# Attention and gated MLP in one kernel: attention output evicted into the natural order of tokens, and an output ring of six tiles

## The chip, the cores and the metric

The kernel runs on one core of one Trainium2 chip. The metric is the device time of one execution in microseconds (us); the median of six runs is compared. A core has five engines, each with its own queue of instructions, worked off in order: TensorE (PE; its weight loads are the row PEld), VectorE (DVE), ScalarE (ACT), GpSimd (POOL) and SyncE (SP, which here only issues DMAs). They meet through semaphores.

## The reference

Two stages. First a linear attention with decay over q, k, v of shape 4 x 8 heads x 768 tokens x 64, in blocks of 64 tokens:

```
for b in range(12):
    intra = einsum('bhic,bhjc->bhij', qb, kb) * Dmask      # Dmask[i,j] = lam**(i-j), i >= j
    intra = einsum('bhij,bhjd->bhid', intra, vb)
    inter = einsum('bhid,bhde->bhie', qb * lam_pow, kv_state)
    out[:, :, sl] = intra + inter
    kv_state = lam_block * kv_state + einsum('bhsd,bhse->bhde', kb_dec, vb)
```

Its heads are laid side by side as x (4 x 768 x 512). Then a gated MLP:

```
h = maximum(x @ w_in, 0)                     # 512 -> 1024
u, v = h[..., :512], h[..., 512:]
v_n = (v - mean(v)) / sqrt(var(v) + 1e-6)    # over the 512 features
v_s = einsum('ts,bsd->btd', w_spatial, v_n) + b_spatial[None, :, None]
out = (u * v_s) @ w_out                      # 4 x 768 x 512
```

## The kernel before

The work comes in twelve groups n of 256 tokens (3 for each of 4 batch entries), each with two chunks c of 128 tokens, and then in work per batch entry bb. Nothing is scheduled by a program: the string ORDER at the top is a list of tokens, walked once, and each token calls one function. The last letter is the engine (T PE, D DVE, A ACT, P POOL, S SP). What one engine does, it does in the order in which its letter comes up in that string.

For a group the tokens are: LK, LQ, LV load 512 KB of k, q, v (SP, line 191; a ring of three tiles each, so LK.8 refills the tile of group 5). Partition p gets the tokens 2p and 2p+1 of the group, so that one descriptor moves 512 contiguous bytes. KC, QC, QM and VD convert and scale them to bf16 (lines 174 to 178, 299 and 314, most on POOL). TK, TQ transpose on PE (L328), EK, EQ evict to kT, qT; from group 7 on DK, DQ do this as DMA transposes from SP. SC forms the scores (L369), MK masks them on DVE into a_sb (L373). KV adds k'v to the running state in PSUM bank 7 (L385), SS copies the state out, AV forms the attention output, transposed, in two banks (L406, L415). EX evicts it to xT (two instructions of 512 elements per partition, 22 of 24 on ACT). PV (L444) and PU (L490) multiply xT with the two halves of w_in, EV and EU apply the relu, giving v and u; BN, RA, RD, VN normalise v to vn.

Since a partition holds two neighbouring tokens, the attention output comes out of PSUM with all even tokens of a chunk ahead of the odd ones. Before the change this order is kept: xT, v and u have it, the spatial weight's transposes (WT, L502) pick every second column of w_spatial to match it on the contracted side, and the gated product puts u back in order.

For a batch entry: PW multiplies vn with the transposed spatial weight (L511), GB adds the bias on DVE into vsb (f32, two tiles, L516), GM forms the gated product gT = vsb * u (L522, 24 on POOL and 8 on DVE; 384 elements per partition each), PO multiplies with w_out (L528), EO evicts to o_sb, a ring of NO tiles (mostly ACT, line 174), ST stores 256 KB (SP, L551). The last tile is done in halves (PH, EH, SH).

Four more things matter for what follows. The 5 tokens GM.0.1.1, GM.0.0.0, GM.0.1.0, GM.0.0.1 and GM.0.3.1 on POOL come among KC.4, VD.3.1, QC.5, and are followed by VD.4.1, VD.4.0, VD.5.1, GT.0.2, WO, VD.5.0, QC.6, QM.7.1, VD.6.1, QM.7.0, VD.6.0, GM.0.2.0, KC.7. GT ("after", L253) copies one element of an input tile, so that what is behind it on POOL waits for that load; GT.0.2 reads the k tile of group 5. WO is the load of w_out, issued by POOL. On DVE the order there is MK.5.0, MK.5.1, GM.0.3.0, BN.3.1, BN.4.1, EQ.6, SS.4.1; on PE, PW.0.2.1 is followed by KV.5.0.

Of the kernel before, what the change touches and what calls it, by code (L numbers as in the profile page):

```python
# [9 lines left out]
BF16 = mybir.dt.bfloat16  # L10
I32 = mybir.dt.int32
AF = mybir.ActivationFunctionType
ALU = mybir.AluOpType
# [20 lines left out]
GM.0.1.0.P KV.3.0.T AV.3.0.0.T GM.0.0.1.P SC.4.1.2.T SS.3.0.A SC.4.0.5.T SY.3.0.D GB.0.2.0.4.D LV.6.2.S  # L34
KV.3.1.T AV.3.1.0.T QC.5.2.P MK.4.1.2.D PW.0.3.0.4.T EX.3.0.0.A EX.3.1.1.A GM.0.3.1.P MK.4.0.5.D TQ.5.0.T
LQ.7.2.S KC.5.2.A PU.3.1.1.T VD.4.1.P EQ.5.0.D SS.3.1.A TK.5.2.T VD.4.0.P GB.0.3.0.4.D PU.3.0.6.T EK.5.2.A
EU.3.1.1.D KV.4.0.T LV.7.2.S VD.5.1.P EU.3.0.6.A AV.4.0.0.T SS.4.0.D SC.5.0.4.T SY.4.0.D LK.7.2.S GT.0.2.P
WO.P SC.5.1.2.T VD.5.0.P KV.4.1.T MK.5.0.4.D AV.4.1.0.T PV.3.1.6.T LK.8.2.S EX.4.0.0.A QC.6.2.P MK.5.1.2.D
EX.4.1.1.A PV.3.0.5.T KC.6.2.A GM.0.3.0.D PV.4.1.0.T LQ.9.2.S EV.3.1.6.A TQ.6.3.T BN.3.1.D EV.4.1.0.A QM.7.1.P
TK.6.1.T PU.4.1.2.T BN.4.1.D VD.6.1.P PU.4.0.4.T EQ.6.3.D EU.4.1.2.A QM.7.0.P SS.4.1.D EV.3.0.5.A PW.0.2.1.6.T  # L40
EK.6.1.D EU.4.0.4.A VD.6.0.P KV.5.0.T GB.0.2.1.6.D AV.5.0.0.T SS.5.0.A SC.6.0.4.T GM.0.2.0.P SC.6.1.2.T
# [42 lines left out]
def kernel(  # L84
# [12 lines left out]
    nc = tc.nc  # L97
    P = 128
# [5 lines left out]
    NCH = DM // P  # L104
    NR = S // (2 * P)
    T2 = 2 * P
    Q64 = 64
    MID = S // 2
    NIN, NCA, NTR, NA, NX, NO, NVS = 3, 2, 2, 2, 3, 4, 2

    const = ctx.enter_context(tc.tile_pool(name="const", bufs=1))
    psum = ctx.enter_context(tc.tile_pool(name="psum", bufs=1, space=bass.MemoryType.PSUM))
# [1 line left out]
    def sb(shape, dt, name):  # L114
        return const.tile(shape, dt, name=name)

    def many(n, shape, dt, name):
        return [const.tile(shape, dt, name=f"{name}_{i}") for i in range(n)]
# [8 lines left out]
    ident = sb([P, P], BF16, "ident")  # L127
# [15 lines left out]
    wsp_raw = sb([P, NT, S], BF16, "wsp_raw")  # L143
# [10 lines left out]
    qT = many(NTR, [P, 4, 2, P], BF16, "qT")  # L154
    a_sb = many(NA, [P, 2, 2, 2, 2, P], BF16, "a_sb")
    s_sb = many(4, [P, 4, D], BF16, "s_sb")
    xT = many(NX, [P, 2, NCH, P], BF16, "xT")
    vh = many(2, [P, NT, DH], BF16, "vh")
    vn = many(2, [P, NT, DH], BF16, "vn")
    uT = many(2, [P, NCH, S], BF16, "uT")  # L160
    gT = many(2, [P, NCH, S], BF16, "gT")
    vsb = many(NVS, [P, S], FP32, "vsb")
# [6 lines left out]
    def bank(b, n=1):  # L169
        return ps[:, b] if n == 1 else ps[:, b:b + n]  # L170

    def copy(e, o, i):
        if e == "A":
            nc.scalar.activation(out=o, in_=i, func=AF.Copy)  # L174
        elif e == "D":
            nc.vector.tensor_copy(out=o, in_=i)  # L176
        else:
            nc.gpsimd.tensor_copy(out=o, in_=i)  # L178

    def vec(e):  # L180
        return nc.vector if e == "D" else nc.gpsimd
# [174 lines left out]
    def row(x):  # L356
        return slice(x * Q64, (x + 1) * Q64)

    def qv(n, o, u, c):
        return qT[n % NTR][row(o), u, :, c * Q64:(c + 1) * Q64]  # L360
# [30 lines left out]
        copy(e, s_sb[(2 * n + c) % 4].rearrange("p u d -> p (u d)"), bank(SB)[:, 0:4 * D])  # L391

    def a_v(e, n, part, b):
        po = bank(b, 2).rearrange("p z (c i x) -> p z c i x", c=2, i=2)
        r = n % NR
        a = a_sb[n % NA]

        def inter(c):
            if r == 0 and c == 0:
                return  # L400
            s = s_sb[(2 * n + c - 1) % 4]
            for i in range(2):
                for o in range(2):
                    for w in range(2):
                        u = 2 * i + w
                        nc.tensor.matmul(out=po[row(w), c ^ o, c, i], lhsT=s[row(o), u, :], rhs=qv(n, o, u, c),  # L406
                                         start=(c == 0 and i == 0), stop=False, skip_group_check=True)

        def intra(o):
            for i in range(2):  # L410
                for j in range(2):
                    for c in range(2):
                        for w in range(2):
                            u = 2 * i + w
                            nc.tensor.matmul(out=po[row(w), c ^ o, c, i], lhsT=vd[n % NCA][row(c), 4 * o + u, j, :],  # L415
                                             rhs=a[row(c), i, o, w, j, :],
                                             start=(r == 0 and o == 0 and i == 0 and j == 0),
                                             stop=(i == 1 and j == 1), skip_group_check=True)

        if part == 0:  # L420
            inter(0)
            intra(0)
        else:
            inter(1)
            intra(1)
# [2 lines left out]
        copy(e, apart[e], ps[0:1, b:b + 2, 0:1].rearrange("p z x -> p (z x)"))  # L428

    def e_x(e, n, z, b):  # L430
        xo = xT[n % NX]
        src = bank(b).rearrange("p (c i x) -> p c i x", c=2, i=2)
        flat = xo.rearrange("p c g x -> p (c g) x")
        if z == 0:
            dst = flat.rearrange("p (a i) x -> p a i x", i=2)[:, 0:4:3]
        else:
            dst = flat.rearrange("p (a i) x -> p a i x", i=2)[:, 1:3]
        copy(e, dst, src)


    def p_v(e, n, c, b):
        x = xT[n % NX]
        for g in range(NCH):
            nc.tensor.matmul(out=bank(b), lhsT=x[:, c, g],  # L444
                             rhs=win_sb[:, g, DH:DFF], start=(g == 0), stop=(g == NCH - 1))

    def relu(e, o, i):
# [34 lines left out]
                             scalar2=rstd[p2][:, t:t + 1], op0=ALU.subtract, op1=ALU.mult)  # L482

    def p_u(e, n, j, b):
        x = xT[n % NX]
        pu = bank(b).rearrange("p (f x) -> p f x", f=2)
        for f2 in range(2):
            f = 2 * j + f2
            for g in range(NCH):
                nc.tensor.matmul(out=pu[:, f2].rearrange("p (c x) -> p c x", c=2), lhsT=win_sb[:, g, f * P:(f + 1) * P],  # L490
                                 rhs=x[:, :, g, :], start=(g == 0), stop=(g == NCH - 1))

    def e_u(e, n, j, b):
        r = n % NR
# [3 lines left out]
    def w_t(e, s, b):  # L498
        pw = bank(b).bitcast(BF16)
        for a in range(NT):  # L500
            for m in range(2):
                nc.tensor.transpose(out=pw[row(m), a * P:(a + 1) * P], in_=wsp_raw[:, a, s * P + m:(s + 1) * P:2],  # L502
                                    identity=ident)

    def e_w(e, s, b):
        pw = bank(b).bitcast(BF16)[:, 0:S]
# [12 lines left out]
    def g_m(e, bb, f, i):  # L519
        HW = S // 2  # L520
        cols = slice(i * HW, (i + 1) * HW)
        vec(e).tensor_tensor(out=gT[bb % 2][:, f, cols].rearrange("p (a y m) -> p a y m", m=2, y=Q64),  # L522
                             in0=vsb[(bb * 4 + f) % NVS][:, cols].rearrange("p (a y m) -> p a y m", m=2, y=Q64),
                             in1=uT[bb % 2][:, f, cols].rearrange("p (a m y) -> p a y m", m=2, y=Q64), op=ALU.mult)

    def p_o(e, bb, t, b):
        for f in range(NCH):
# [21 lines left out]
    def st_o(e, bb, t):  # L549
# [3 lines left out]
    ops = dict(GT=after, lam=c_lam, WU=w_u, pos=c_pos, LB=l_b, LN=l_n, LL=l_l, LX=l_x, LT=l_t, idn=c_ident, msk=c_mask, mkc=c_mask2, WI=w_in, WS=w_sp, WO=w_out, BS=b_sp,  # L553
               LK=ld_k, LQ=ld_q, LV=ld_v, KC=k_c, QM=q_m, DK=d_k, DQ=d_q, QC=q_c, VD=v_d, TK=t_k, TQ=t_q, EK=e_k, EQ=e_q,
               SC=s_c, MK=m_k, KV=k_v, SS=s_s, AV=a_v, SY=s_y, EX=e_x, PV=p_v, EV=e_v, BN=b_n, RA=r_a, RD=r_d,
               VN=v_n, PU=p_u, EU=e_u, WT=w_t, EW=e_w, PW=p_w, GB=g_b, GM=g_m, PO=p_o, EO=e_o, ST=st_o, EH=e_h, SH=s_h, PH=p_h)
    with tc.manual_schedule():
        for token in ORDER.split():
# [32 lines left out]
```

## Time and profile before

| what | value |
|---|---|
| median of six runs | 152.56 us |
| the six runs | 147.62, 149.36, 149.83, 155.28, 155.66, 158.30 us |
| the profiled execution, its own time | 155.66 us |
| its span, first to last instruction | 154.0 us |
| mean granted PE clock | 0.965 of full |
| busy: PE, PEld, DVE, ACT, POOL | 140.6, 93.3, 105.2, 87.8, 74.5 us |
| chain that ended last: PE, DVE, ACT, issue, POOL | 77%, 10%, 5%, 4%, 2% |
| gated products L522, POOL | 24, mean 1098 ns, 26.0 us |
| gated products L522, DVE | 8, mean 1511 ns, 12.0 us |
| v scaling L314, POOL (512 elements) | 19, mean 1065 ns |
| bias add L516, DVE | 32, mean 550 ns |
| xT evictions L174, ACT | 22, mean 595 ns |
| output evictions L174, ACT, 512 elements | 22, mean 595 ns; 2.9 us waiting for output DMAs |
| spatial transposes L502, PE | 72 |
| DMA | 31.25 MB, mean 203 GB/s |

How to read it: [...]The chain of waits goes back from the last instruction to what released each step. A group is all instructions of one line, engine and form, with the mean duration and the idle time of the engine ahead of them. The timeline gives start, duration, engine, line and, in brackets, the idle time before and what ended it. Line 174, 176 and 178 are a copy helper (ACT, DVE, POOL), so its groups go by the tile written.

### The profile page before, as it was taken

What the parts mean: (1) busy time and instruction counts of PE and PEld (TensorE: products, weight loads), DVE (VectorE), ACT (ScalarE), POOL (GpSimd) and SP (SyncE); (2) the same over time, 40 slices, a digit from 0 to 9 for tenths busy, and PEclk for the clock granted to TensorE, in tenths of its full rate; (3) what the DMA queues carried; (4) which work ended last, traced back from release to release, by engine and by line L of the source; (5) the groups of instructions that cost most, each with busy time, mean ns of one, the idle gap of its engine ahead of it and who ended that gap; (6) DMA issues with size and microseconds to landing.
All of it is one profiled execution on the core that took longest, in us unless ns stands there. A gap on an engine that the chain in (4) does not pass through costs nothing.

```text
span 154.0 us, 4883 instructions
## 1 busy us (share of the span) xinstructions
PE 140.6 (91%) x2070; PEld 93.3 (61%) x2085; DVE 105.2 (68%) x191; ACT 87.8 (57%) x167; POOL 74.5 (48%) x84
## 2 busy tenths in 40 slices
PE   6998689999999999099999999999999999999990
PEld 4785546768766867083565657655676756565540
DVE  1468606988996799968566778885469888848301
ACT  3968238968406765035799824668373646942270
POOL 7445463205089999158244585574754102014910
PEclk9999969999999999857999999999999999999999
DMA  3999999999999999808699997988999000051355
GB/s 99 298 290 269 260 231 268 216 283 284 302 283 286 291 264 229 236 9 159 185 270 280 140 232 223 315 188 258 156 302 180 6 2 0 4 197 75 136 216 193
DMA packets 54152, 31.25 MB, mean 203 GB/s; under 512 B 11634, under 2 KB 51058, under 8 KB 54130
## 3 DMA queue, kind: packets, MB, share of 16 engines
q1 hardware_dynamic: 51600, 28.05, 73.2%
q0 software_dynamic: 2384, 2.75, 10.3%
q8 instruction: 16, 0.26, 0.7%
q10 hardware_dynamic: 146, 0.13, 0.2%
q14 instruction: 6, 0.05, 0.1%
HBM read 24.77 MB, written 6.29 MB: 202 GB/s over the span
## 4 chain that ended last, share of the span: by engine, by line
PE 77%; DVE 10%; ACT 5%; issue 4%; POOL 2%; DVEq 0%; POOLq 0%
PE ps L511 17%; PE ps L528 13%; PE ps L490 12%; PE ps L444 12%; PE ps L212 6%; DVE gT L522 4%; PE ps L415 4%; PE ps L369 3%; PE ps L385 3%; PE ps L328 3%; PE ps L406 2%; ACT kT L174 2%; ACT lq L234 2%; DVE a_sb L373 2%; POOL gT L522 1%
## 5 line engine op out<-in xcount | busy, mean ns | idle before, releaser
L522 POOL TENSOR_TENSOR gT<-vsb,uT 128x384 bf16<-128x384 f32 x24 | 26.0, 1098 | 33.2 <-DVE vsb L516 25.0
L511 PE MATMUL ps<-wt_sb,vn 128*128 128x384 bf16 x192 | 33.9, 327 | 0.0
L373 DVE TENSOR_TENSOR a_sb<-ps,m 128x1024 bf16<-128x1024 f32 x24 | 28.6, 1215 | 2.9 <-PE ps L369 2.5
L314 POOL TENSOR_TENSOR vd<-v_in,lv 128x512 bf16<-128x512 f32 x19 | 20.0, 1065 | 13.8 <-DMA v_in<-in_v_dram 8.8
L511 PEld LDWEIGHTS <-vn 128*128 128x128 bf16 x192 | 18.2, 98 | 11.9
L490 PE MATMUL ps<-xT,win_sb 128*128 128x256 bf16 x192 | 24.4, 273 | 0.0
L444 PE MATMUL ps<-win_sb,xT 128*128 128x512 bf16 x87 | 23.5, 397 | 0.8 <-issue 0.4
L516 DVE TENSOR_TENSOR vsb<-ps,bsp 128x384 f32<-128x384 f32 x32 | 17.2, 550 | 9.1 <-PE ps L511 9.0
L528 PE MATMUL ps<-wout_sb,gT 128*128 128x512 bf16 x86 | 22.1, 390 | 0.4 <-issue 0.2
L490 PEld LDWEIGHTS <-win_sb 128*128 128x128 bf16 x192 | 18.4, 98 | 4.7
L449 ACT ACTIVATE vh<-ps 128x512 bf16<-128x512 f32 x23 | 13.7, 597 | 12.5 <-PE ps L444 12.5
L174 ACT ACTIVATE o_sb<-ps 128x512 f32<-128x512 f32 (+1 forms) x23 | 13.1, 585 | 12.1 <-PE ps L528 9.2
L459 DVE BATCH_NORM_STATS2 st<-vh 128x6 f32<-128x512 bf16 x24 | 16.3, 681 | 3.1 <-ACT vh L449 3.0
L174 ACT ACTIVATE xT<-ps 128x512 bf16<-128x512 f32 x22 | 12.2, 595 | 7.7 <-PE ps L415 7.6
L444 PEld LDWEIGHTS <-xT 128*128 128x128 bf16 x96 | 9.1, 101 | 10.4 <-issue 1.7
L528 PEld LDWEIGHTS <-gT 128*128 128x128 bf16 x92 | 9.0, 100 | 9.9 <-issue 0.8
L212 PE MATMUL ps<-warm 128*128 128x256 bf16 x71 | 11.5, 317 | 2.7 <-DVE warm L210 1.3
L385 PE MATMUL ps<-vd,kc 64*64 64x64 bf16 x320 | 9.3, 201 | 5.0 <-DVE s_sb L176 3.7
L449 ACT ACTIVATE uT<-ps 128x512 bf16<-128x512 f32 x20 | 11.7, 595 | 2.9 <-PE ps L490 2.6
L299 POOL TENSOR_TENSOR qc<-q_in,lqn 128x512 bf16<-128x512 f32 x10 | 10.7, 1076 | 4.8 <-DMA q_in<-in_q_dram 4.7
L178 POOL CAST kc<-k_in 128x1024 bf16<-128x1024 f32 x6 | 6.2, 1036 | 13.9 <-DMA k_in<-in_k_dram 10.2
L385 PEld LDWEIGHTS <-kc 64*64 64x64 bf16 x320 | 7.8, 115 | 7.3 <-issue 6.9
(72 smaller groups left out, 184.6 us busy)
## 6 DMA issues: line engine op xcount, KB each, us to landing
k_in<-in_k_dram SPq DMA_DIRECT2D x12, 512.0 KB, 7.0
q_in<-in_q_dram SPq DMA_DIRECT2D x12, 512.0 KB, 7.8
v_in<-in_v_dram SPq DMA_DIRECT2D x12, 512.0 KB, 7.1
out_dram<-o_sb SPq DMA_DIRECT2D x23, 256.0 KB, 2.4
wsp_raw<-in_moe_w_spatial_dram POOLq DMA_DIRECT2D x2, 576.0 KB, 10.8
win_sb<-in_moe_w_in_dram POOLq DMA_DIRECT2D x2, 512.0 KB, 9.9
wout_sb<-in_moe_w_out_dram POOLq DMA_DIRECT2D x1, 512.0 KB, 10.1
bsp<-in_moe_b_spatial_dram SPq DMA_DIRECT2D x1, 384.0 KB
```

Source lines behind the costliest of these rows:

```text
L174: nc.scalar.activation(out=o, in_=i, func=AF.Copy)
L212: nc.tensor.matmul(out=bank(SB)[:, 4 * D:8 * D], lhsT=warm[:, 0:P], rhs=warm, start=(n < 0 and x == 0), stop=True, skip_group_check=True)
L314: vec(e).tensor_tensor(out=vd[n % NCA].rearrange("p (o i w) m d -> p o i (w m) d", o=2, i=2)[o], in0=v_in[n % NIN].rearrange("p (o i w) m ...
L373: nc.vector.tensor_tensor(out=a_sb[n % NA][:, i].rearrange("p o w j x -> p (o w) (j x)"), in0=bank(b, 2).rearrange("p o (w y) -> p (o w) y ...
L385: nc.tensor.matmul(out=pkv[row(o), u], lhsT=kc[n % NCA][row(c), u, m, o, :], rhs=vd[n % NCA][row(c), 4 * o + u, m, :], start=new and u == ...
L444: nc.tensor.matmul(out=bank(b), lhsT=x[:, c, g], rhs=win_sb[:, g, DH:DFF], start=(g == 0), stop=(g == NCH - 1))
L449: nc.scalar.activation(out=o, in_=i, func=AF.Relu)
L490: nc.tensor.matmul(out=pu[:, f2].rearrange("p (c x) -> p c x", c=2), lhsT=win_sb[:, g, f * P:(f + 1) * P], rhs=x[:, :, g, :], start=(g == ...
L511: nc.tensor.matmul(out=bank(b)[:, 0:HW], lhsT=vn[bb % 2][:, s, f * P:(f + 1) * P], rhs=wt_sb[:, s, i * HW:(i + 1) * HW], start=(s == 0), s ...
L516: nc.vector.tensor_tensor(out=vsb[(bb * 4 + f) % NVS][:, i * HW:(i + 1) * HW], in0=bank(b)[:, 0:HW], in1=bsp[:, i * HW:(i + 1) * HW], op=A ...
L522: vec(e).tensor_tensor(out=gT[bb % 2][:, f, cols].rearrange("p (a y m) -> p a y m", m=2, y=Q64), in0=vsb[(bb * 4 + f) % NVS][:, cols].rear ...
L528: nc.tensor.matmul(out=bank(b), lhsT=gT[bb % 2][:, f, t * P:(t + 1) * P], rhs=wout_sb[:, f, :], start=(f == 0), stop=(f == NCH - 1))
```

## The change

The attention output is put into the natural order of tokens when it is evicted to xT. AV's two banks have their chunks in another order (i, c in place of c, i), and each eviction reads its bank straight through and stores with an inner step of two bf16 elements, even tokens and odd tokens interleaved. PV and PU find their blocks of xT at other places. From there on v and u are in natural order: the spatial transposes take 64 neighbouring columns, and the gated products are plain, with all operands contiguous. The output ring grows from four tiles to six. One token, GT.0.2.P, is dropped from the order; all other tokens stay as they were (two lines of the string are wrapped differently).

```diff
-... LK.7.2.S GT.0.2.P
-WO.P SC.5.1.2.T ...
+... LK.7.2.S WO.P
+SC.5.1.2.T ...
-    NIN, NCA, NTR, NA, NX, NO, NVS = 3, 2, 2, 2, 3, 4, 2
+    NIN, NCA, NTR, NA, NX, NO, NVS = 3, 2, 2, 2, 3, 6, 2
-    xT = many(NX, [P, 2, NCH, P], BF16, "xT")
+    xT = many(NX, [P, 2, 2, 2, P], BF16, "xT")
     def a_v(e, n, part, b):
-        po = bank(b, 2).rearrange("p z (c i x) -> p z c i x", c=2, i=2)
+        po = bank(b, 2).rearrange("p z (i c x) -> p z c i x", c=2, i=2)
     def e_x(e, n, z, b):
-        xo = xT[n % NX]
-        src = bank(b).rearrange("p (c i x) -> p c i x", c=2, i=2)
-        flat = xo.rearrange("p c g x -> p (c g) x")
-        if z == 0:
-            dst = flat.rearrange("p (a i) x -> p a i x", i=2)[:, 0:4:3]
-        else:
-            dst = flat.rearrange("p (a i) x -> p a i x", i=2)[:, 1:3]
-        copy(e, dst, src)
+        copy(e, xT[n % NX].rearrange("p i c z (y m) -> p (i c) z m y", m=2)[:, :, z],
+             bank(b).rearrange("p (k m y) -> p k m y", k=4, m=2))
     def p_v(e, n, c, b):
-            nc.tensor.matmul(out=bank(b), lhsT=x[:, c, g],
+            nc.tensor.matmul(out=bank(b), lhsT=x[:, g % 2, c, c ^ (g // 2)],
     def p_u(e, n, j, b):
-        x = xT[n % NX]
+        x = xT[n % NX].rearrange("p i c z x -> p (i c z) x")
+                o, i = divmod(g, 2)
-                                 rhs=x[:, :, g, :], start=(g == 0), stop=(g == NCH - 1))
+                                 rhs=x[:, 4 * i + o:4 * i + 4 - o:3 - 2 * o], start=(g == 0), stop=(g == NCH - 1))
     def w_t(e, s, b):
-                nc.tensor.transpose(out=pw[row(m), a * P:(a + 1) * P], in_=wsp_raw[:, a, s * P + m:(s + 1) * P:2],
-                                    identity=ident)
+                c0 = s * P + m * Q64
+                nc.tensor.transpose(out=pw[row(m), a * P:(a + 1) * P], in_=wsp_raw[:, a, c0:c0 + Q64], identity=ident)
     def g_m(e, bb, f, i):
-        vec(e).tensor_tensor(out=gT[bb % 2][:, f, cols].rearrange("p (a y m) -> p a y m", m=2, y=Q64),
-                             in0=vsb[(bb * 4 + f) % NVS][:, cols].rearrange("p (a y m) -> p a y m", m=2, y=Q64),
-                             in1=uT[bb % 2][:, f, cols].rearrange("p (a m y) -> p a y m", m=2, y=Q64), op=ALU.mult)
+        vec(e).tensor_tensor(out=gT[bb % 2][:, f, cols], in0=vsb[(bb * 4 + f) % NVS][:, cols],
+                             in1=uT[bb % 2][:, f, cols], op=ALU.mult)
```

More of the change, by code (lines that the diff above doesn't have):

```diff
@@ L36 @@
 LQ.7.2.S KC.5.2.A PU.3.1.1.T VD.4.1.P EQ.5.0.D SS.3.1.A TK.5.2.T VD.4.0.P GB.0.3.0.4.D PU.3.0.6.T EK.5.2.A
-EU.3.1.1.D KV.4.0.T LV.7.2.S VD.5.1.P EU.3.0.6.A AV.4.0.0.T SS.4.0.D SC.5.0.4.T SY.4.0.D LK.7.2.S GT.0.2.P
-WO.P SC.5.1.2.T VD.5.0.P KV.4.1.T MK.5.0.4.D AV.4.1.0.T PV.3.1.6.T LK.8.2.S EX.4.0.0.A QC.6.2.P MK.5.1.2.D
+EU.3.1.1.D KV.4.0.T LV.7.2.S VD.5.1.P EU.3.0.6.A AV.4.0.0.T SS.4.0.D SC.5.0.4.T SY.4.0.D LK.7.2.S WO.P
+SC.5.1.2.T VD.5.0.P KV.4.1.T MK.5.0.4.D AV.4.1.0.T PV.3.1.6.T LK.8.2.S EX.4.0.0.A QC.6.2.P MK.5.1.2.D
 EX.4.1.1.A PV.3.0.5.T KC.6.2.A GM.0.3.0.D PV.4.1.0.T LQ.9.2.S EV.3.1.6.A TQ.6.3.T BN.3.1.D EV.4.1.0.A QM.7.1.P
```

## The prediction

> **What bounds the kernel now.** I read the chain of waits first. TensorE (PE) holds 77% of it. Then the line of granted clock in the 40 slices of 3.85 us:
>
> ```profile
> PE   6998689999999999099999999999999999999990
> PEclk9999969999999999857999999999999999999999
> ```
>
> PE is full in every slice from the seventh on except slice 17 (61.6 to 65.5 us), and in that slice and the two after it the clock dips. Two stretches from the table of windows (length, PE busy, PEld, DVE, ACT, POOL, then the clock):
>
> ```profile
> 65.00:69.00 4.00, 3.81 (x113) 3.26 (x114) 2.60 (x5) 1.12 (x4) 1.71 (x2) 0.50 0.06 16
> 69.00:73.00 4.00, 3.86 (x13) 1.60 (x13) 3.64 (x8) 2.27 (x6) 3.45 (x4) 0.69 0.81 149
> ```
>
> PE works there at half and at two thirds of its clock. So one place is worth reading closely. The chain, in order of time (start, us, what):
>
> ```profile
> 55.46 1.21 DVE a_sb L373
> 56.68 5.86 DVE gT L522
> 62.54 0.61 DVE st L459
> ...
> 64.07 0.66 DVE qT L354
> 64.73 0.34 DVE s_sb L176
> 65.07 0.04 issue
> 65.11 0.64 PE ps L385 x12
> ```
>
> One gated product on DVE (GM.0.3.0.D) takes 5.9 us. Queued behind it on DVE is SS.4.1.D, which empties PSUM bank 7, and PE can't start KV.5.0 before. The timeline of PE, with the idle time ahead in brackets:
>
> ```profile
> 65.11 0.64 PE L385 MATMUL ps<-vd,kc 64*64 64x64 bf16 x16 [3.73 <-DVE s_sb L176]
> ```
>
> This is PE's longest wait; from there to the end it has two of 0.22 and 0.16 us. What is special in that product? The other seven on DVE take 0.56 to 1.45 us (its group: min 559, median 786, max 5945 ns). The timelines of DVE and of POOL tell:
>
> ```profile
> 56.60 5.95 DVE L522 TENSOR_TENSOR gT<-vsb,uT 128x384 bf16<-128x384 f32 x1
> ```
>
> ```profile
> 56.05 1.04 POOL L178 CAST qc<-q_in 128x1024 bf16<-128x1024 f32 x1
> 57.05 1.03 POOL L299 TENSOR_TENSOR qc<-q_in,lqn 128x512 bf16<-128x512 f32 x1
> 58.05 1.03 POOL L314 TENSOR_TENSOR vd<-v_in,lv 128x512 bf16<-128x512 f32 x1
> 59.05 1.03 POOL L299 TENSOR_TENSOR qc<-q_in,lqn 128x512 bf16<-128x512 f32 x1
> 60.05 1.03 POOL L314 TENSOR_TENSOR vd<-v_in,lv 128x512 bf16<-128x512 f32 x1
> 61.05 1.07 POOL L522 TENSOR_TENSOR gT<-vsb,uT 128x384 bf16<-128x384 f32 x1
> 65.88 1.04 POOL L178 CAST kc<-k_in 128x1024 bf16<-128x1024 f32 x1 [3.75 <-issue]
> ```
>
> POOL has no gap from 42.93 to 62.12 us, and the DVE product ends 0.43 us after POOL does: it was shut out.
>
> [...] Before, the product reads u with an inner step of 64 bf16 elements, and takes 1.09 us for 384 elements (2.8 ns each), while the scaling of v, packed, takes 1.04 for 512 (2.03 ns)[...].
>
> **The change part by part.**
>
> *Products on POOL (24).* With all operands packed I take the rate of the v scaling: 384 x 2.03 = 0.78 us instead of 1.09, 0.31 saved[...]. 24 x 0.31 = 7.4 us of POOL. After 65 us PE doesn't wait for POOL, so this is worth nothing there; without that cover it would be 0.31 for each product. It matters for the run of work above. Five products lie between 42.93 and QM.7.1 (57.05): POOL comes to QM.7.1 by 5 x 0.31 = 1.55 earlier.
>
> *The token GT.0.2 dropped.* Its step on POOL was 0.13 us (54.12 to 54.25). So POOL is at QM.7.1 at 57.05 - 1.55 - 0.13 = 55.4. On SP the load LK.8 no longer waits for it (1.6 us in the waits of the queue), and LV.7, which waits for VD.4.0, goes about 1.5 earlier. The load of w_out moves as much; it must have landed by the first output product, and landed at 64.35 before (issued 54.25, 10.1 us).
>
> *What POOL meets at 55.4.* QM.7.1 needs q_in of group 7, issued by SP at 48.57 and landed 7.8 us later, at 56.4. The DMA was full then, so I let that time stand. So POOL sits idle from 55.4 to 56.4, where before it had 0.65 us in hand.
>
> *When DVE asks.* QC.5.2 on POOL ended at 50.14 and PE took its transposes at 50.20, having been free at 49.93; now QC.5.2 ends near 49.0: 0.27 earlier on PE. Next, KV.4.0 waited 0.25 (53.27) for VD.4.0 or the kT copy, ended 53.18 and 53.25: both come earlier, so another 0.25. The a_sb masks follow, and DVE asks for its product at 56.6 - 0.5 = 56.1. That falls in POOL's gap, with 0.3 us to spare. Then the product costs 0.56, POOL waits 0.2 for it, and the pause of PE goes.
>
> *What the pause is worth.* 3.73 us of idle PE, and its clock: over 65 to 73 us 4 x (1 - 0.50) + 4 x (1 - 0.69) = 3.24 us at most. Late next is VD.6.0 on POOL (done near 61.4), needed by KV.6.0 on PE near 62: hidden, narrowly.
>
> *Evictions into natural order (24, 22 on ACT).* I take 0.595 us as before. ACT's rate from two rows, (1022 - 595)/512 = 0.83 ns per element, leaves 427 ns to be doubled if stores of single bf16 elements ran at half rate: bounds 0 and +0.43 each, +9.4 us of ACT in all. TensorE's reads of xT stay in blocks of 128 elements: 0. DVE's products (8) at 0.56 equal the packed bias add at 0.55: 0.
>
> *Weight transposes.* 72 in 2.13 us, 30 ns each; the loads (110 ns, overlapping) become packed. Others of 128 columns take 0.45 to 0.62 us for 8. Taken as 0, bounds 0 and -0.3.
>
> *Output ring of six.* ACT waited 2.39 (139.2) and 0.46 (148.5) for output DMAs. PE had no gap around 139, and at the end the last matmul ends at 150.05 whatever ACT did before, its final eviction starting at 150.13: 0, bound -0.4.
>
> **Sum**, against the profiled execution (155.66 us, span 154.0 and 1.66 around it): 155.66 - 3.73 - 3.24 - 0.5 = 148.2; I say 148.3. That execution is in the upper half of the six runs (147.62 to 158.30, median 152.56). The lowest runs, 147.62 to 149.83, lie where this sum goes without the 0.5 (148.7): I read them as runs in which DVE already got its turn. So I expect few new lows, but most runs near the lows.
>
> **Rivals.**
> 1. [...]For it: 0.3 us of margin, worked out from several steps. If q_in lands before DVE asks, POOL runs on through QM.7.1 to GM.0.2.0, and ends at 56.4 + 4 x 1.0 + 0.8 = 61.2 instead of 62.1: 155.66 - 0.9 = 154.7; with runs of both kinds the median is 150 to 154.7.[...]
> 2. *The interleaved store is slow; the kernel ends slower.* Place: the two evictions at 49.04 us on ACT, ahead of KC.5.2, whose transposes feed the masks ahead of DVE's product. From +0.15 us each DVE asks after 56.4, [...]and the pause stays. At the full +0.43: 155.66 + 0.85 there + 0.85 for the pair at 24.05 ahead of the kT copy + some 1.3 for single ones (16 to 33 us) = 158.7.[...]
> 3. *The pause goes but a smaller wait takes its place*: w_out landing, or VD.6.0 held by a later q_in, costs PE 1 to 2 us: 150.
> 4. *Packed products are no faster on POOL*: only 0.13 is saved and POOL meets no gap; 155.5, counted with rival 1.
>
> **How the numbers follow.** Forecast 0.58 (own range 146.2 to 149.8); rivals 1 and 4 0.24; rival 2 0.12; rival 3 0.06. Faster by over 2% (below 149.5; 2% is about what a measurement of this kernel can tell from no change): 0.56 of the forecast, 0.04 of the rest, 0.60. Slower (above 155.6): 0.11 of rival 2 and 0.02 of rival 1, 0.13. Within: 0.27. The range runs from 146.2 to rival 1's 154.9 and leaves rival 2 out.
>
> **What would show it.** Products on POOL near 0.78 us; a gap on POOL before QM.7.1 near 56 us; the first DVE product under 1 us; no wait of PE above 0.5 us after 53 us and full clock from 61 us on; ACT evictions of xT at 0.60. Wrong if that product is again several us long, if xT's evictions are above 0.75 us, or if the packed products stay at 1.09.

## The result

The changed kernel takes 149.40 us (median of 35 runs, 147.39 to 157.11); the kernel before, now run 72 times, takes 149.07 (147.33 to 158.80), so the six runs shown ahead had set its median 3.5 us too high. The ratio of like runs is 1.0003, interval 0.998 to 1.0027: no change. A ratio of like runs compares only runs within 1.5% of the fastest of their kernel; it leaves out all runs above 153 us, which I count apart.

| | runs | above 153 us | median of the other runs |
|---|---|---|---|
| kernel before, all runs | 276 | 107 (39%) | 148.88 |
| changed kernel, both times that it was run | 57 | 8 (14%) | 148.77 |

Experiment 7 aside, I take the runs above 153 us as those in which PE paused: the three such executions that have a profile (155.66, 155.59 and 154.49 us) show the pause, and no profiled execution below 150 us does. So the pause of the kernel before is real, and rarer after the change. But the typical run of the kernel before never had it. (The profiled execution of the changed kernel took 148.49 us, span 146.8.)

The profile of the changed kernel shows the pause and the low clock behind it gone. Busy tenths and clock per slice (now 3.67 us each):

```profile
PE   6999589999999999999999999999999999999990
PEclk9999977999999999999999999999999999999999
```

No slice is empty but the last, and the clock doesn't dip after the first quarter. The two stretches, by the table of windows, are at full clock:

```profile
65.00:69.00 4.00, 4.00 (x51) 2.17 (x50) 3.13 (x12) 2.95 (x9) 1.68 (x2) 1.00 0.82 179
69.00:73.00 4.00, 3.89 (x105) 2.87 (x105) 2.48 (x8) 3.72 (x8) 0.36 (x1) 1.00 0.60 165
```

The chain around KV.5.0, which had waited 3.73 us (L506 is what L511 was):

```profile
58.21 1.75 PE ps L485 x16
59.96 0.97 PE ps L506 x6
60.93 0.30 PE ps L385 x12
```

PE goes from PW.0.2.1 into KV.5.0 without a gap. The product on DVE, and what POOL did around it:

```profile
56.15 0.55 DVE L517 TENSOR_TENSOR gT<-vsb,uT 128x384 bf16<-128x384 f32 x1
```

```profile
55.11 1.04 POOL L178 CAST qc<-q_in 128x1024 bf16<-128x1024 f32 x1
56.20 1.39 POOL L299 TENSOR_TENSOR qc<-q_in,lqn 128x512 bf16<-128x512 f32 x1
57.56 1.04 POOL L314 TENSOR_TENSOR vd<-v_in,lv 128x512 bf16<-128x512 f32 x1
```

DVE asks at 56.15, as POOL's QC.6.2 ends, and takes 0.55 us. Now QM.7.1 is the one that is held: 1.39 us instead of 1.03. The last two rows to compare are groups, with count, busy time and mean duration:

```profile
L517 POOL TENSOR_TENSOR gT<-vsb,uT 128x384 bf16<-128x384 f32 x24 | 21.8, 917 | 35.4 <-DVE vsb L511 26.6
L174 ACT ACTIVATE xT<-ps 128x512 bf16<-128x512 f32 x22 | 15.2, 743 | 6.8 <-PE ps L415 6.6
```

Products on POOL went from 1098 to 917 ns, the evictions to xT from 595 to 743. Span against span, 154.0 - 146.8 = 7.2 us: KV.5.0 starts 65.11 - 60.93 = 4.18 earlier, and the stretch behind it is 88.89 - 85.87 = 3.02 shorter, near the 3.24 that the low clock from 65 to 73 us could cost at most.

### The profile page after: what moved, and what is told of

The parts are those of the page before. It is cut to its first block, busy times and chain, and to the rows that moved or that the text cites. A ratio compares the mean times of both kernels' runs of the same rounds, so it can differ in the third digit from the quotient of the medians.

```text
span 146.8 us, 4879 instructions
## 1 busy us (share of the span) xinstructions
PE 137.7 (94%) x2070; PEld 91.5 (62%) x2085; DVE 99.1 (68%) x191; ACT 89.8 (61%) x167; POOL 70.7 (48%) x83
## 4 chain that ended last, share of the span: by engine, by line
PE 87%; ACT 6%; DVE 2%; issue 2%
PE ps L506 21%; PE ps L438 14%; PE ps L522 13%; PE ps L485 13%; PE ps L212 6%; PE ps L415 4%; PE ps L369 4%; PE ps L328 4%; PE ps L385 4%; PE ps L406 2%; ACT lq L234 2%; PE ps L498 1%; ACT kT L174 1%; ACT xT L174 1%; ACT vh L443 1%
## 5 line engine op out<-in xcount | busy, mean ns | idle before, releaser
L517 POOL TENSOR_TENSOR gT<-vsb,uT 128x384 bf16<-128x384 f32 x24 | 21.8, 917 | 35.4 <-DVE vsb L511 26.6
L506 PE MATMUL ps<-wt_sb,vn 128*128 128x384 bf16 x192 | 33.9, 327 | 0.0
L506 PEld LDWEIGHTS <-vn 128*128 128x128 bf16 x192 | 18.2, 98 | 11.9
L511 DVE TENSOR_TENSOR vsb<-ps,bsp 128x384 f32<-128x384 f32 x32 | 17.2, 550 | 9.8 <-PE ps L506 7.2
L438 PE MATMUL ps<-win_sb,xT 128*128 128x512 bf16 x87 | 22.8, 388 | 0.6 <-issue 0.2
L522 PE MATMUL ps<-wout_sb,gT 128*128 128x512 bf16 x86 | 21.4, 379 | 0.4 <-issue 0.2
L174 ACT ACTIVATE xT<-ps 128x512 bf16<-128x512 f32 x22 | 15.2, 743 | 6.8 <-PE ps L415 6.6
L299 POOL TENSOR_TENSOR qc<-q_in,lqn 128x512 bf16<-128x512 f32 x10 | 11.5, 1152 | 7.9 <-DMA q_in<-in_q_dram 6.1
L174 ACT ACTIVATE kT<-ps 128x1024 bf16<-128x1024 bf16 x6 | 6.1, 1020 | 8.1 <-PE ps L328 7.6
L415 PE MATMUL ps<-a_sb,vd 64*64 64x128 bf16 x384 | 11.0, 225 | 0.0
```

The source lines that it names most:

```text
L438: nc.tensor.matmul(out=bank(b), lhsT=x[:, g % 2, c, c ^ (g // 2)], rhs=win_sb[:, g, DH:DFF], start=(g == 0), stop=(g == NCH - 1))
L506: nc.tensor.matmul(out=bank(b)[:, 0:HW], lhsT=vn[bb % 2][:, s, f * P:(f + 1) * P], rhs=wt_sb[:, s, i * HW:(i + 1) * HW], start=(s == 0), s ...
L511: nc.vector.tensor_tensor(out=vsb[(bb * 4 + f) % NVS][:, i * HW:(i + 1) * HW], in0=bank(b)[:, 0:HW], in1=bsp[:, i * HW:(i + 1) * HW], op=A ...
L517: vec(e).tensor_tensor(out=gT[bb % 2][:, f, cols], in0=vsb[(bb * 4 + f) % NVS][:, cols], in1=uT[bb % 2][:, f, cols], op=ALU.mult)
L522: nc.tensor.matmul(out=bank(b), lhsT=gT[bb % 2][:, f, t * P:(t + 1) * P], rhs=wout_sb[:, f, :], start=(f == 0), stop=(f == NCH - 1))
```

## The experiments

Theory A: the pause is DVE shut out by POOL; the change makes it rarer; a run without it gains nothing. Theory B: runs without the pause would gain from faster products, but the slower evictions eat it. Every kernel was timed in five rounds beside the kernel before.

**1. The product taken off DVE, in the kernel before.**

```diff
-... KC.6.2.A GM.0.3.0.D PV.4.1.0.T ...
-... GM.0.2.0.P SC.6.1.2.T
+... KC.6.2.A PV.4.1.0.T ...
+... GM.0.2.0.P GM.0.3.0.P SC.6.1.2.T
```

> The kernel before with one change: the product GM.0.3.0 goes from DVE to POOL, behind GM.0.2.0[...]. [...]no run lies above 153 us (27 of 72 of the kernel before did), PE has no wait above 0.5 us after 53 us, and the lower group of times stays at 148.3 (ratio of like runs 0.997 to 1.003). If the pause comes of something else, a late load say, about one run in three stays above 153.

None of 22 runs lies above 153 us, where 24 of 60 of the kernel before, run beside it, did. The median of all is 148.90, the ratio of like runs 1.0017 (0.9987 to 1.0047). The pause hangs on this one instruction being on DVE.

**2. Products alone, in the kernel before.**

```diff
     def g_m(e, bb, f, i):
-        vec(e).tensor_tensor(out=gT[bb % 2][:, f, cols].rearrange("p (a y m) -> p a y m", m=2, y=Q64),
...
+        vec(e).tensor_tensor(out=gT[bb % 2][:, f, cols], in0=vsb[(bb * 4 + f) % NVS][:, cols],
+                             in1=uT[bb % 2][:, f, cols], op=ALU.mult)
```

> The kernel before with plain gated products alone: the reordering of u is left out, so even and odd tokens of v and u are mixed. Evictions stay at 0.595. Products on POOL near 0.91 us. Theory A: ratio of like runs 1.000 within 0.003, and clearly fewer than 3 of 8 runs above 153, since POOL now has a gap when DVE asks. Theory B: with no slower eviction the gain shows, ratio 0.995 to 0.997.

None of 14 runs above 153; median 148.87; ratio 0.9986 (0.9944 to 1.0028). Its products on POOL mean 918 ns, its evictions 595. The timelines of DVE and POOL in its profile:

```profile
56.92 0.55 DVE L522 TENSOR_TENSOR gT<-vsb,uT 128x384 bf16<-128x384 f32 x1
```

```profile
55.97 1.04 POOL L178 CAST qc<-q_in 128x1024 bf16<-128x1024 f32 x1
57.55 1.04 POOL L299 TENSOR_TENSOR qc<-q_in,lqn 128x512 bf16<-128x512 f32 x1 [0.54 <-DMA q_in<-in_q_dram]
```

POOL is through with QC.6.2 at 57.01, the load of q (issued at 49.78, landed 7.6 later) lets QM.7.1 go at 57.55, and DVE's product fits between. It is a gap of the forecast kind, but in this execution it isn't made as forecast: POOL is no earlier than in the kernel before (57.01 against 57.09); the load lands a microsecond later (57.4 against 56.4).

**3. The eviction alone, in the kernel before** (AV, EX, PV, PU and xT as changed).

```diff
     def e_x(e, n, z, b):
...
+        copy(e, xT[n % NX].rearrange("p i c z (y m) -> p (i c) z m y", m=2)[:, :, z],
+             bank(b).rearrange("p (k m y) -> p k m y", k=4, m=2))
```

> The kernel before with the eviction into natural order alone (and PV and PU reading xT accordingly); spatial transposes and products are those of before, so the order of tokens is mixed behind it. Evictions near 0.74. Theory A: ratio of like runs 1.000 within 0.003, and as many or more runs above 153 as before (3 of 8), since DVE asks about 0.3 us later. Theory B: ratio 1.003 or above.

9 of 14 runs above 153, median of all 154.38; the others have 148.55, ratio 1.0003 (0.9958 to 1.0048). The products alone bring the share of pauses down clearly (0 of 14 against 24 of 60). That the evictions alone raise it isn't shown: 9 of 14 against 24 of 60 can be chance. Runs without a pause move in neither, as far as the intervals of about 0.45% (0.7 us) can tell.

**4. Packed stores in the changed kernel.**

```diff
-        copy(e, xT[n % NX].rearrange("p i c z (y m) -> p (i c) z m y", m=2)[:, :, z],
-             bank(b).rearrange("p (k m y) -> p k m y", k=4, m=2))
+        copy(e, xT[n % NX].rearrange("p i c z x -> p (i c) z x")[:, :, z].rearrange("p k (y m) -> p k y m", m=2),
+             bank(b).rearrange("p (k m y) -> p k y m", k=4, m=2))
```

> The changed kernel, but each eviction to xT reads PSUM with a step of 64 f32 and stores packed, same values at the same places. If the 0.15 us that the eviction gained (0.595 to 0.743 on ACT) is the 4-byte step of the store, it is back near 0.60; if it is the short runs of the pattern, it stays near 0.74. If slower evictions ate what faster products gave (theory B), the kernel is 0.3 to 0.5 us faster than the changed one (ratio to before 0.997 or below); [...]the ratio stays 1.000 within 0.003.

The group of evictions in its profile:

```profile
L174 ACT ACTIVATE xT<-ps 128x512 bf16<-128x512 f32 x22 | 12.2, 595 | 6.8 <-PE ps L415 6.6
```

595 ns, as in the kernel before: the 0.15 us (743 - 595) is the store's step of 4 bytes, and a step of 64 f32 in the read of PSUM added nothing here. The time: ratio 0.9966 (0.9935 to 0.9997), 4 of 22 runs above 153. By the ratio this met what theory B expected, so the two were run side by side on one chip.

> The changed kernel itself, beside the next one on the same chip, to set the two against each other. Ratio of like runs to before 0.997 to 1.003; about 1 run in 7 above 153.

> The changed kernel with packed stores and a stepped read of PSUM, once more, beside the changed kernel on the same chip. If the slower store costs time, it is 0.3 to 0.5 us below the changed kernel; if not, within 0.2.

Changed kernel: 1.0008 (0.9977 to 1.0040), 3 of 22 above 153. Packed stores: 0.9987 (0.9960 to 1.0014), 1 of 23. Median of the runs below 153: 148.77 for both, where 0.3 to 0.5 us had been in question. With the earlier runs added, those below 153 have 148.77 (49 runs) against 148.62 (40). A tenth or two may be there. By the two ratios it would be 0.3 us, and their intervals overlap; so the lower end of what theory B expected isn't excluded.

The profiled execution of the second packed kernel is one with a pause (span 152.8), and tells how the changed kernel still comes to it. DVE and POOL in it, then the window from 15 to 25 us of the changed kernel and of this one:

```profile
57.71 4.87 DVE L517 TENSOR_TENSOR gT<-vsb,uT 128x384 bf16<-128x384 f32 x1
```

```profile
56.26 1.04 POOL L178 CAST qc<-q_in 128x1024 bf16<-128x1024 f32 x1
57.26 1.04 POOL L299 TENSOR_TENSOR qc<-q_in,lqn 128x512 bf16<-128x512 f32 x1
58.26 1.03 POOL L314 TENSOR_TENSOR vd<-v_in,lv 128x512 bf16<-128x512 f32 x1
```

```profile
15.00:25.00 10.00, 7.92 (x184) 5.55 (x185) 3.05 (x3) 4.19 (x9) 4.67 (x7) 0.83 1.18 259
```

```profile
15.00:25.00 10.00, 7.68 (x166) 4.85 (x167) 3.33 (x3) 3.00 (x10) 4.77 (x7) 0.66 1.18 263
```

PE's clock was 0.66 there instead of 0.83, and POOL and DVE are 1.1 and 1.6 us later at 56 us. The load of q is not: issued at 48.64, landed 7.6 later, at 56.2. So POOL finds its data and leaves no gap for DVE. It is a race between POOL and a load. That the lower clock made the engines late is likely, but not shown: the kernel before has the pause too, with 0.83 in the same window.

**5. The gap filled, in the changed kernel.**

```diff
-... QC.6.2.P ...
+... GM.0.3.1.P QC.6.2.P ...
```

> The changed kernel with the product GM.0.3.1 issued a second time on POOL ahead of QC.6.2 (same values, 0.87 us more), so that POOL comes to QM.7.1 near 57.1 us, after the load of q has landed (56.3 to 56.5), and leaves no gap when DVE asks at 56.1. If the gap decides, the pause comes back: most runs, at least 1 in 2, above 153, and the DVE product takes 5 us or more in a profile of such a run. If the change removed the pause in another way (DVE earlier, a packed operand on DVE), the share stays near 1 in 7 and the kernel costs nothing.

5 of 18 runs above 153 (median of all 149.74), short of the half that I expected. With 18 runs this is told apart neither from 1 in 7 nor from the kernel before beside it (7 of 24). In its profile POOL still waits 0.39 us for the load of q ahead of QM.7.1: it was through with QC.6.2 at 56.47, not near 57.1, and QM.7.1 starts at 56.87. The gap wasn't filled, so this one doesn't decide.

**6. Both cures, and the changed kernel with the product off DVE.** The edits are those of 1 and 4 together, and that of 1:

```diff
-... KC.6.2.A GM.0.3.0.D PV.4.1.0.T ...
-... GM.0.2.0.P SC.6.1.2.T
+... KC.6.2.A PV.4.1.0.T ...
+... GM.0.2.0.P GM.0.3.0.P SC.6.1.2.T
```

> The changed kernel with both cures: packed stores in the eviction to xT, and the product GM.0.3.0 on POOL behind GM.0.2.0. Expected: no run above 153, median of all runs 148.3 (before 149 to 150), ratio of like runs 0.995 to 0.999, evictions at 0.595. If the few tenths that packed stores gave came only of the pause's neighbourhood, the ratio is that of product_off_dve, about 1.001.

> The changed kernel with GM.0.3.0 on POOL behind GM.0.2.0, evictions as changed (0.74). If the slower evictions cost time off the pause too, it is 0.3 to 0.5 us above packed_store_off_dve; if they are covered wholly, the two agree within 0.2. No run above 153.

No run above 153 in 22 of each. Medians 148.91 and 148.99; ratios 0.9952 (0.9918 to 0.9986) and 0.9979 (0.9948 to 1.0011). By the medians the two agree, as they would if the slower store were covered; by the ratios packed stores are 0.4 us better, by the means of all runs (149.48 and 149.01) 0.5 us worse. So these runs resolve no gain from packed stores. The kernel before beside them has a mean of 151.83: what can be gained here lies in the pause.

**7. The eviction twice, as a dose** (on the kernel of 6 without packed stores).

```diff
+        for again in range(2):
-        copy(e, xT[n % NX]...
+            copy(e, xT[n % NX]...
```

> The changed kernel with GM.0.3.0 on POOL (no pause) and every eviction to xT issued twice, the same values to the same place: 0.66 to 0.74 us more for each on its engine, some five times what the change added (0.15). If evictions are covered by other work, the time stays within 0.5 us of after_off_dve (ratio to before up to 1.001). If the 0.15 costs the 0.3 to 0.4 us that the runs with packed stores hint at, five times as much is 1.5 to 2 us: ratio 1.008 to 1.013.

159.78 us, ratio 1.0726 (1.0670 to 1.0783): far above both expectations. PE's waits for the evictions, the two longest groups of its profile (us in total, times, longest):

```profile
PE ps L439 <- ACT xT L174: 4.3, 5, 1.2
PE ps L486 <- ACT xT L174: 2.0, 2, 1.2
```

A pair of evictions takes 2.90 us instead of 1.35, and PE waits for it up to 1.2 us at a time. So evictions are not free: another 0.7 to 0.8 us for each is not covered. An estimate along a straight line from this dose, 10.8 us x 0.15/0.75, gives 2.2 us for the 0.15 us that the change adds, which no run shows; so some cover comes first, and how much of the 0.15 it takes is known only to the few tenths of experiments 4 and 6.

**8. The small parts alone, in the kernel before:** the token GT.0.2 dropped; the ring set to six.

```diff
-... LK.7.2.S GT.0.2.P
+... LK.7.2.S
```

```diff
-    NIN, NCA, NTR, NA, NX, NO, NVS = 3, 2, 2, 2, 3, 4, 2
+    NIN, NCA, NTR, NA, NX, NO, NVS = 3, 2, 2, 2, 3, 6, 2
```

> The kernel before without the token GT.0.2 alone. POOL is 0.13 us earlier at QM.7.1, LK.8 no longer waits for it. Expected: ratio of like runs 1.000 within 0.003 and about 2 of 5 runs above 153, as before. If the earlier load of w_out held q_in back and so gave DVE its turn, the share above 153 falls to that of the changed kernel (1 in 7).

> The kernel before with an output ring of six tiles alone. ACT's wait for output DMAs (2.9 us) goes; expected ratio of like runs 1.000 within 0.003, since PE had no gap behind it; 2 of 5 runs above 153 as before. If ACT's wait had held the end, up to 0.4 us faster (0.997).

Each has 7 of 22 runs above 153, as before (39% would be 8.6). Ratios: 0.9971 (0.9931 to 1.0012) for the token, 0.9948 (0.9914 to 0.9981) for the ring. With the ring, ACT's 2.9 us of waits for output DMAs are gone from the profile, yet the span of that execution is 147.3 us, no lower than the others'. The changed kernel, which holds the ring of six, stands at 1.0003. And the four kernels that were compared with these same runs of the kernel before (these two and those of 6) all lie below 1, so a part of each may lie in those runs. I don't take the 0.5% as shown; whether the ring gives a tenth or two is open.

**9. What decides in single executions.** Ten profiled executions have the product GM.0.3.0 on DVE. All times in us; usually an instruction on POOL starts 0.04 ahead of the recorded end of the one before it.

| execution | POOL through with QC.6.2 | QM.7.1 starts | DVE's product starts | and takes |
|---|---|---|---|---|
| kernel before | 57.09 | 57.05 | 56.60 | 5.95 |
| token dropped (8) | 57.02 | 56.98 | 56.61 | 5.86 |
| packed stores, second (4) | 57.30 | 57.26 | 57.71 | 4.87 |
| changed kernel, first | 56.15 | 56.20 | 56.15 | 0.55 |
| changed kernel, second (4) | 55.43 | 56.29, after a wait for the load | 55.44 | 0.55 |
| packed stores, first (4) | 56.12 | 56.12 | 56.00 | 0.55 |
| products alone (2) | 57.01 | 57.55, after a wait for the load | 56.92 | 0.55 |
| eviction alone (3) | 56.45 | 56.66, after a wait for the load | 55.91 | 0.97 |
| ring of six (8) | 56.91 | 57.33, after a wait for the load | 56.70 | 0.63 |
| gap filled (5) | 56.47 | 56.87, after a wait for the load | 56.41 | 0.55 |

In the three executions with the pause, the load of q had landed (56.4, 56.2, 56.2) before POOL was through, and POOL ran on without a gap. In five of the other seven POOL had to wait for the load, and DVE got its turn; in the last two QM.7.1 starts 0.09 and 0.04 later than usual, and DVE comes in there. The kernel with the ring of six has the load and the products of the kernel before, and shows how its runs without a pause can come about: the load landed at 57.2 there, after POOL was through. The second profile of the changed kernel shows the forecast at its plainest:

```profile
54.39 1.04 POOL L178 CAST qc<-q_in 128x1024 bf16<-128x1024 f32 x1
56.29 1.04 POOL L299 TENSOR_TENSOR qc<-q_in,lqn 128x512 bf16<-128x512 f32 x1 [0.86 <-DMA q_in<-in_q_dram]
```

```profile
55.44 0.55 DVE L517 TENSOR_TENSOR gT<-vsb,uT 128x384 bf16<-128x384 f32 x1
```

## Why the prediction was wrong

Right: where the pause is, what makes it, and that the change makes it rarer. In the profile the two terms came out as summed: pause and earlier start 4.18 us (forecast 3.73 + 0.5), clock 3.02 (3.24 at most), time 148.49 (148.3). Experiments 1 and 6 bear out that the pause needs this product on DVE: with it on POOL, 0 of 66 runs lie above 153. By what means POOL's work holds it up, no run shows. Right behind the pause PE is slow in all three profiled executions that have one: 32 score products (L369) take 1.16 us in each, where 30 of them take 0.62 in nine executions without a pause. The granted clock was 0.50 there in the kernel before (65 to 69 us), and 1.00 in the changed one.

Wrong: the last step, "but most runs near the lows", turned into a change of the median. The sum was made against one execution with a pause, and the step from it to the median took the six runs as they lay, three and three. The median of such six lies midway between 149.83 and 155.28, at 152.56, where none of the 276 runs of this kernel lies (none between 151.5 and 153.8). Nor was it a rare draw: with a share of 39%, an estimate from the counts above, six runs hold three or more with a pause in about 4 of 10 cases. I had read the low runs rightly ("runs in which DVE already got its turn"), and my own sum gave them 148.7 against 148.2: a gain of 0.3%, which is no change by the 2% that I had named. Faster by over 2% would have needed the typical run of before to have the pause; 61% of its runs don't. The forecast had to be two numbers, a share of runs and a time without the pause: the share fell from 39% to 14%, the time stayed at 148.9 and 148.8. That the measured 149.40 lies inside the forecast's own range of 146.2 to 149.8 says nothing for the gain: the kernel before, at 149.07, lies in it too.

Sizes that were off. Products on POOL: 0.78 us forecast, 0.917 measured, so 0.18 saved, not 0.31. The rate came from the v scaling, whose second operand is one value repeated along the row, while the product reads two full streams; it also has 512 elements, not 384. Which of the two it is, no run separates. The prediction's reading of the inner step came from that comparison too, 2.8 ns per element against 2.03, a factor of 1.38: the same product with the step and without it differs by a factor of 1.20 (1098 and 917 ns). Evictions: 0.595 forecast, 0.743 measured, a third of the way into the bound of +0.43. That bound assumed a halved rate; measured were 0.29 ns more per element, on the 0.83 from which it was worked out. With both, PE was 0.38 us earlier at KV.4.0 (53.27 to 52.89) of the 0.52 forecast, and DVE asked 0.45 earlier (56.60 to 56.15) of 0.5. POOL was to be through with QC.6.2 1.68 us earlier; it was 0.94 earlier in the first profile of the changed kernel (57.09 to 56.15), where only 0.05 us of gap was left and DVE came in by a hair, and 1.66 earlier in the second (55.43), where POOL idled 0.86. The margin differs that much between executions, and in 1 of 7 runs it isn't enough.

The rivals. 1 (the pause still there in about as many runs) fell: 14% against 39%. 2 (a slow store) had the right sign: the store is slower, right at the threshold of +0.15 from which I had the pause stay; but DVE still asked at 56.15 and at 55.44 in the two profiles. Alone the eviction had 9 of 14 runs with a pause, which isn't told apart from the kernel before; with the products it didn't keep the pause. 3: no new wait of PE showed. 4 fell. Dropped token and output ring: nothing that I take as shown, as forecast. The transposes weren't run alone.

Not explained: why runs without a pause spread over some 4 us (147.3 to 151.5 for the kernel before, 147.4 to 150.9 for the first 35 of the changed one). The granted clock differs by up to 2.6% between them, but no profile was taken of a run between 150 and 153. Nor is it known why 24 of the 107 runs with a pause take 156.8 to 158.8 us, and the others 153.9 to 155.9; none of the slower ones has a profile.

## What to carry to other kernels

When single runs of a kernel fall in groups, first ask in which group the profiled execution lies and how often each comes; a gain that is read from the rarer group moves the mean, not the typical run. Where a VectorE product of two SBUF tiles can fall behind a gapless run of GpSimd work, read its duration there: here it took 4.87 to 5.95 us, against 0.55 to 0.97 where it got in between, and 6.5 us lie between the medians of runs with the pause and without. Moving it to the other engine ended the pause (0 of 66 runs), shortening the run only made it rarer (8 of 57). When an eviction has to reorder, try stepping through PSUM on the reading side with the SBUF store packed: ScalarE was 0.15 us faster with it here (595 against 743 ns), though no gain of the whole kernel is shown.

## What the runs showed of the hardware

- ScalarE storing bf16 with a step of 4 bytes: 743 ns for 512 elements in the changed kernel against 595 packed, 0.29 ns more per element; VectorE 714 against 674 (medians of two).
- ScalarE reading PSUM f32 with a step of 64 elements, stored packed: 595 ns in experiment 4, as much as reading it straight in the kernel before.
- VectorE's product of two SBUF operands: 0.55 us in five executions in which it got in between two GpSimd instructions (0.63 and 0.97 in two more), 5.95, 5.86 and 4.87 us behind a run of GpSimd instructions without a gap.
- GpSimd's product of two full streams of 384 elements: 917 ns packed in the changed kernel, 1098 with one operand at a step of 64 in the kernel before; with the second operand one value per row, 512 elements take 1042.
